# Linear attention and a SwiGLU block in fp32: k^T v of the next block in two visits per up phase

## The chip, the cores and the metric

The kernel runs on one core of one Trainium2 chip. The metric is device time in microseconds, median of three runs: 1023.67 (1023.01 to 1025.28). The trace shown below comes from an execution with a span of 1021.4 us. All data are fp32.

## What is computed

The reference, cut to what matters: a linear attention without softmax and with an RMS norm per head, then a gated feed-forward block on the result, read as 4608 tokens of width 512.

```python
# q, k, v: (8, 8, 576, 64);  g_norm: (64,);  w_gate, w_val: (512, 1536);  w_out: (1536, 512)
kv  = np.einsum('bhsd,bhse->bhde', k, v)
o   = np.einsum('bhsd,bhde->bhse', q, kv)
x   = o / np.sqrt(np.mean(o * o, axis=-1, keepdims=True) + 1e-6) * g_norm
x   = x.transpose(0, 2, 1, 3).reshape(4608, 512)
g   = x @ w_gate
out = (g / (1 + np.exp(-g)) * (x @ w_val)) @ w_out
```

## The kernel before

The 4608 tokens are cut into nine blocks of 512. A sequence has 576 tokens, so a block of tokens lies across two sequences, and blocks of k^T v (one for each of the eight sequences) are numbered as the blocks are. Each block n goes through an up phase (x times w_gate and w_val, then silu and the product h) and a down phase (h times w_out). The attention of block n+1 is worked into the phases of block n: k^T v in the up phase (`kv`, L305 to L323), q times k^T v, norm and the turning of x in the down phase (`steps`, L502).

The products of the feed-forward block are not the plain ones. From block 1 on, each is split into 2 x 2 pieces and done with seven products in place of eight (Winograd's form), with sums of operands and results on VectorE, GpSimd and ScalarE. `CHAIN` (L533) lists the seven; products 1, 6, 7 and 4 share a PSUM tile b, 5 and 3 a tile c, and 2 has a tile a. Block 0 has the plain products (`plain_up`, L1023). Block 1 has one level in the up phase (class `Up`, L587, products at L565). From block 2 on (`DEEP`, L540) the up phase has two levels (class `Inner`, L660, products at L728): 12 units, each of an outer product or two, whose weight leaves are read from DRAM into tiles t of a pool of nine (`Stream`, L787, loads at L809). In block 1 VectorE also makes these leaves (`leaf_steps`, L829) and SyncE stores them (L837). The down phase has one level in all blocks (class `Down`, L855, at L565), with products in the order 1, 6, 5, 7, 2, 4, 3 or 1, 5, 6, 7, 2, 4, 3 (L999).

k^T v of one block: eight heads in four pairs, nine slices of 64 rows each, products of 64 x 64 (L316). `kv(0)` is pairs 0 and 1, `kv(1)` is pairs 2 and 3; each has 9 x 2 x 2 = 36 products. Both write two PSUM tiles m, and after `kv(1)` ScalarE copies them out (L323). k and v come through tiles ld (a pool of four, which q uses too): the loads for `kv(1)` (`load_kv(1)`, L266) are in the source behind `kv(0)`.

In the up phase of block n (L968) a loop runs over the units, and after a third and two thirds of them calls `fill[4]` and `fill[8]`, which are `third` (L1109) and `two_thirds` (L1113). This is the order of the source. The order in the queue of each engine is decided when the program is built: a scheduler takes the instructions that its own estimate holds ready, so a group of products need not stay together or stand where the source has it. `tc.issue_after(ins)` binds what is traced inside it to be queued behind `ins` on `ins`'s own engine; it adds no wait on a semaphore.

In the program of before the products at L316 stand on TensorE as follows; "down" is the down phase of block n-1, between its products 2 and 4, "third" and "two thirds" are the places of the source. The 72 products for block 1 stand together ahead of the down phase of block 0 and are outside this table and outside the change.

| up phase n (k^T v of block n+1) | visits, in products |
|---|---|
| 1 | 17 down, 19 third, 36 two thirds |
| 2 | 17 down, 19 third, 29 in the unit before two thirds, 7 two thirds |
| 3, 4, 5 | 17 down, 19 third, 36 two thirds |
| 6 | 17 down, 8 and 11 in the first unit, 36 two thirds |

Phases 7 and 8 have none, since there are eight sequences.

Of the kernel before, what the change touches and what calls it, by code (L numbers as in the profile page):

```python
# [18 lines left out]
def kernel(  # L19
# [41 lines left out]
    nc = tc.nc  # L61

    B, H, S, D = q.shape
# [55 lines left out]
    class Words:  # L119
# [12 lines left out]
        def __init__(self, src, shape):  # L132
            self.raw = ld_pool.tile([P, LD], U32, name="ld")[:, 0 : 2 * BLK]
            dst = self.raw.rearrange("p (a b) -> p a b", a=shape[0])
            self.sent = nc.sync.dma_start(out=dst, in_=src)
            self.shape = shape
            self.begun = False
# [55 lines left out]
    class Att:  # L193
# [111 lines left out]
        def kv(self, g):  # L305


            if self.n == B:
                return
            if g == 0:  # L310
                self.kv_ps = [m_psum.tile([P, 2, D], F32, name="m") for _ in range(2)]
            for c in range(KT):
                for r in range(2):
                    k, v = self.k[2 * g + r], self.v[2 * g + r]
                    for u in range(2):
                        nc.tensor.matmul(  # L316
                            self.kv_ps[r][u * D : (u + 1) * D, g, :], lhsT=k[:, u, c, :], rhs=v[:, u, c, :],
                            start=(c == 0), stop=(c == KT - 1),
                        )
            if g == 1:  # L320
                dst = kvs[self.n % 3].rearrange("p (g r) d -> p r g d", r=2)
                for r in range(2):
                    nc.scalar.copy(out=dst[:, r], in_=self.kv_ps[r])  # L323
# [220 lines left out]
    class Quad:  # L544
# [11 lines left out]
        def multiply(self, p):  # L556
            name, first = CHAIN[p]
            if first:
                tiles = [PSUMS[name].tile([P, 2, HB], F32, name=name) for _ in range(1 + (name in self.apart))]
                self.ps[name], self.apart[name] = tiles[0], tiles[-1]  # L560
            banks = self.ps[name], self.apart[name]
            for e, i in self.order(p):
                lhsT, rhs = self.operands(p, e, i)

                nc.tensor.matmul(  # L565
                    banks[e][:, e], lhsT=lhsT, rhs=rhs, start=first and i == 0 and (e == 0 or banks[0] is not banks[1]),
                    stop=i == self.steps - 1, skip_group_check=True,
                )
            getattr(self, f"after{p}", lambda: None)()
# [90 lines left out]
    class Inner:  # L660
# [58 lines left out]
        def multiply(self, p):  # L719
            if p == 1:  # L720
                self.begin()
            name, first = CHAIN[p]
            if first:
                self.ps[name] = PSUMS[name].tile([P, 2, 2, P], F32, name=name)
            ps = self.ps[name][:, 0 : len(self.outers)]
            for i, o in enumerate(self.outers):
                for f in range(2):
                    nc.tensor.matmul(  # L728
                        ps[:, i, f], lhsT=self.weight(o, p, f), rhs=self.operand(o, p),
                        start=first and (i, f) == (0, 0), stop=True, skip_group_check=True,  # L730
                    )
            if p in self.ADDED:
                e, q = self.ADDED[p]
                dst = self.dst[:, :, :, e, q]
                add(nc.vector, dst, ps, dst)
            else:
                e, q = self.MADE[p]
                dst = self.dst[:, :, :, e, q]
                if self.onto:
                    add(nc.vector, dst, ps, self.onto(e, q))  # L740
                else:
                    nc.scalar.copy(out=dst, in_=ps)  # L742
            if p in (2, 7, 3, 4):
                getattr(self, f"made{self.g}", lambda *_: None)(p, e, q)
            stream.pump()
# [196 lines left out]
    class Ffn:  # L942
        def __init__(self, n, att):
            self.n, self.att = n, att
            self.h = h_pool.tile([P, NF, BLK], F32, name="h")
            self.ps, self.leaf_room, self.ended, self.owed = {}, None, None, None

            self.making, self.later, self.latest = [], [], []

        def store(self, o, t, columns=slice(None)):  # L950
            rows = out[BLK * self.n : BLK * (self.n + 1), columns].rearrange("(t p) d -> p t d", t=T)
            nc.sync.dma_start(out=rows[:, t : t + o.shape[1], :], in_=o)
# [15 lines left out]
        def up(self, fill):  # L968

            self.s1 = s_pool.tile([P, NP, HB], F32, name="s1")  # L970
            units = []
            for d in range(NP // 2):
                if self.n < DEEP:
                    units += [Up(self, 2 * d), Up(self, 2 * d + 1)]
                else:
                    shared = {}
                    units += [Inner(self, d, g, shared) for g in range(4)]
            units[0].prepare()
            last = None
            for i, this in enumerate(units):  # L980
                if i + 1 < len(units):
                    units[i + 1].prepare()
                for unit, p in this.sequence(last):
                    if unit:
                        unit.multiply(p)
                        self.make(4)
                last = this
                fill.get(12 * (i + 1) // len(units), lambda: None)()
            self.down_ = Down(self)
            self.down_.turn_t(5)  # L990
            for unit, p in last.sequence(None):
                if unit is None:
                    last.multiply(p)
# [86 lines left out]
    for n in range(NB):  # L1080
        ffn = Ffn(n, blocks[n])
        nxt = blocks[n + 1] if n + 1 < NB else None
# [23 lines left out]
                nxt.kv(g)  # L1106
        else:

            def third():  # L1109
                nxt.kv(0)  # L1110
                nxt.load_kv(1)

            def two_thirds():  # L1113
                nxt.kv(1)
                if nxt.n == 2:
                    for i in range(2):
                        nxt.load_q(i)

            fill = {4: third, 8: two_thirds} if nxt else {}
            if n == DEEP:  # L1120
                for a, at in enumerate((1, 2, 3, 5)):
# [50 lines left out]
```

## Time and profile before

| what | value |
|---|---|
| time, median of 3 | 1023.67 us |
| span of the traced execution | 1021.4 us |
| TensorE busy | 1006.0 us, 98% |
| VectorE busy | 701.1 us, 69% |
| GpSimd, ScalarE busy | 369.0 and 227.9 us |
| records of L316 on TensorE | 1008, two for each product, 217 to 268 ns each, up to four at once |
| granted TensorE clock | 1.000 |
| HBM traffic | 138.02 MB read, 22.41 MB written, 157 GB/s over the span |

The duration of a record of TensorE is that of one product from its issue to its end, and products overlap in the pipeline. What a group costs is therefore read from starts: the time from the start of one group to the start of the next. In the timeline, instructions of one line and form are merged, with the count behind; a group's printed duration runs to the end of its last product and overlaps the next group. Idle time is printed in brackets with what ended it, and only where the records leave a gap. The busy share of TensorE is an upper bound for its work for the same reason: records of a product that waits inside the array count as busy.

### The profile page before, as it was taken

The numbers are of one execution on the slowest core, as the hardware profiler recorded it, in microseconds if no ns is written. First come the engines' busy times: TensorE is split into PE (matmuls) and PEld (weight loads), VectorE is DVE, ScalarE is ACT, GpSimd is POOL, SyncE is SP. The second block draws the span as 40 slices with busy tenths as digits, with TensorE's granted clock in tenths as the row PEclk, the third lists the DMA queues.
The fourth block names the chain that finished last, engine by engine and source line by source line (L and its number), as shares of the span: only waits on it lengthen the run. The fifth ranks groups of instructions, "written<-read, shape, count | busy, mean of one in ns | idle before, by whom it ended". The sixth has DMA issues, their size and how long they took to land.

```text
span 1021.4 us, 21409 instructions
## 1 busy us (share of the span) xinstructions
PE 1006.0 (98%) x8522; PEld 897.1 (88%) x8522; DVE 701.1 (69%) x1169; ACT 227.9 (22%) x353; POOL 369.0 (36%) x280
## 2 busy tenths in 40 slices
PE   6999999999999999999999999999999999999998
PEld 4544688888999989998999899988998999989997
DVE  2999688998665946685558566665669466946661
ACT  2765112121211221121121211111121211221110
POOL 0000263534055503561246315630555045513670
PEclk9999999999999999999999999999999999999999
DMA  8689643767888377845686568636772766066601
GB/s 237 203 255 271 124 77 108 187 165 156 250 210 255 60 176 203 252 92 129 209 238 144 96 195 247 177 60 201 231 199 46 177 195 190 22 167 201 191 27 42
DMA packets 273845, 170.26 MB, mean 167 GB/s; under 512 B 150609, under 2 KB 241873, under 8 KB 273745
## 3 DMA queue, kind: packets, MB, share of 16 engines
q1 hardware_dynamic: 238800, 164.42, 59.3%
q10 hardware_dynamic: 34880, 4.46, 2.7%
q8 instruction: 68, 1.11, 0.4%
q14 instruction: 33, 0.26, 0.1%
q0 software_dynamic: 64, 0.00, 0.0%
HBM read 138.02 MB, written 22.41 MB: 157 GB/s over the span
## 4 chain that ended last, share of the span: by engine, by line
PE 90%; DVE 6%; DMA 2%; issue 1%; ACT 1%; SPq 0%; DVEq 0%; ACTq 0%
PE b L728 26%; PE b L565 19%; PE c L728 13%; PE c L565 10%; PE a L728 6%; PE a L565 5%; PE b L1032 4%; PE c L1032 4%; PE m L316 2%; PE m L361 1%; DVE r L112 1%; DVE xi L112 1%; DVE r L111 1%; DMA h<-in_v_dram 1%; DVE t L112 1%
## 5 line engine op out<-in xcount | busy, mean ns | idle before, releaser
L111 POOL TENSOR_TENSOR r<-r 128x256 f32<-128x256 f32 (+1 forms) x105 | 110.8, 1061 | 300.9 <-DVE r L111 272.2
L111 DVE TENSOR_TENSOR r<-b,r 128x512 f32<-128x512 f32 (+1 forms) x273 | 161.9, 606 | 65.5 <-PE b L728 60.1
L112 POOL TENSOR_TENSOR t<-wo 128x512 f32<-128x512 f32 x81 | 114.5, 1438 | 212.4 <-DVE wo L111 102.9
L111 DVE TENSOR_TENSOR r<-c,r 128x512 f32<-128x512 f32 (+1 forms) x179 | 108.5, 617 | 89.0 <-PE c L728 54.8
L728 PE MATMUL b<-x,t 128*128 128x128 f32 x1092 | 151.3, 276 | 0.0
L111 DVE TENSOR_TENSOR r<-a,r 128x512 f32<-128x512 f32 (+1 forms) x99 | 62.5, 631 | 113.4 <-PE a L565 70.7
L728 PEld LDWEIGHTS b<-x,t 128*128 128x128 f32 x1092 | 136.5, 192 | 0.8
L728 PE MATMUL c<-xi,t 128*128 128x128 f32 x840 | 112.4, 276 | 0.4 <-DVE xi L111 0.4
L113 POOL TENSOR_TENSOR h<-r 128x1024 f32<-128x1024 f32 (+1 forms) x40 | 82.3, 2072 | 76.9 <-DVE r L111 73.9
L728 PEld LDWEIGHTS c<-xi,t 128*128 128x128 f32 x840 | 102.9, 192 | 0.5 <-DVE xi L111 0.5
L565 PE MATMUL b<-wo,h 128*128 128x256 f32 x432 | 100.1, 383 | 0.1
L565 PE MATMUL b<-t,h 128*128 128x256 f32 x432 | 96.9, 381 | 0.0
L565 PEld LDWEIGHTS b<-t,h 128*128 128x128 f32 x432 | 81.6, 190 | 11.3 <-issue 0.2
L565 PEld LDWEIGHTS b<-wo,h 128*128 128x128 f32 x432 | 79.9, 190 | 13.1 <-DVE h L113 2.5
L742 ACT COPY r<-b 128x512 f32<-128x512 f32 x63 | 36.9, 585 | 211.6 <-PE b L728 211.6
L728 PE MATMUL b<-xi,t 128*128 128x128 f32 x588 | 79.8, 276 | 0.0
L728 PEld LDWEIGHTS b<-xi,t 128*128 128x128 f32 x588 | 72.4, 192 | 0.0
L728 PE MATMUL b<-x,wg 128*128 128x128 f32 x336 | 52.7, 279 | 0.2 <-DVE x L112 0.2
L728 PE MATMUL b<-x,wv 128*128 128x128 f32 x336 | 51.4, 276 | 0.0
L565 PE MATMUL a<-wo,h 128*128 128x256 f32 x216 | 48.3, 379 | 0.0
L565 PE MATMUL c<-t,s 128*128 128x256 f32 x216 | 48.1, 380 | 0.0
L565 PE MATMUL c<-wo,h 128*128 128x256 f32 x216 | 48.1, 379 | 0.0
(133 smaller groups left out, 1565.7 us busy)
## 6 DMA issues: line engine op xcount, KB each, us to landing
t<-w SPq DMA_DIRECT2D x336, 256.0 KB, 3.6
out_dram<-r SPq DMA_DIRECT2D x17, 512.0 KB, 3.1
ld<-in_k_dram SPq DMA_DIRECT2D x26, 288.0 KB, 5.2
ld<-in_v_dram SPq DMA_DIRECT2D x26, 288.0 KB, 5.9
ld<-in_moe_w_gate_dram SPq DMA_DIRECT2D x12, 512.0 KB, 4.8
ld<-in_moe_w_val_dram SPq DMA_DIRECT2D x12, 512.0 KB, 4.7
ld<-in_moe_w_out_dram SPq DMA_DIRECT2D x12, 512.0 KB, 4.9
w<-t SPq DMA_DIRECT2D x18, 256.0 KB, 3.0
```

The source lines that it names most:

```text
L111: add = lambda e, o, a, b: e.tensor_tensor(out=o, in0=a, in1=b, op=OP.add)
L112: sub = lambda e, o, a, b: e.tensor_tensor(out=o, in0=a, in1=b, op=OP.subtract)
L113: mul = lambda e, o, a, b: e.tensor_tensor(out=o, in0=a, in1=b, op=OP.mult)
L316: nc.tensor.matmul(self.kv_ps[r][u * D : (u + 1) * D, g, :], lhsT=k[:, u, c, :], rhs=v[:, u, c, :], start=(c == 0), stop=(c == KT - 1),)
L361: self.multiplied = nc.tensor.matmul(self.ps[i][u][p : p + D, t, j, :], lhsT=self.qt[rows, 2 * i + t, j, p : p + D], rhs=kvs[b % 3][rows, ...
L565: nc.tensor.matmul(banks[e][:, e], lhsT=lhsT, rhs=rhs, start=first and i == 0 and (e == 0 or banks[0] is not banks[1]), stop=i == self.ste ...
L728: nc.tensor.matmul(ps[:, i, f], lhsT=self.weight(o, p, f), rhs=self.operand(o, p), start=first and (i, f) == (0, 0), stop=True, skip_group ...
L742: nc.scalar.copy(out=dst, in_=ps)
L1032: nc.tensor.matmul(t, lhsT=w[f // 2][:, i, P * (f % 2) : P * (f % 2 + 1)], rhs=x[:, i, of], start=(i == 0), stop=(i == NS - 1),)
```

## The change

k^T v of the next block is to be kept in two visits per up phase. Two bounds are put on the queue of TensorE. `visit(g)` traces `kv(g)` inside an `issue_after` on the last product that was traced before it (`ffn.multiplied`, set at L565 and L728), so its products can't be queued ahead of that one. And where the visited block is one with k^T v (`nxt.n < B`), the last product of `kv(g)` (`positions`) is kept in `ffn.visited`, and the next unit's product in `up` is traced inside an `issue_after` on it, so it can't be queued ahead of the end of the visit. Nothing is computed differently.

```diff
@@ kv
-                        nc.tensor.matmul(
+                        self.positions = nc.tensor.matmul(
@@ Quad.multiply
-                nc.tensor.matmul(
+                self.ffn.multiplied = nc.tensor.matmul(
@@ Inner.multiply
-                    nc.tensor.matmul(
+                    self.ffn.multiplied = nc.tensor.matmul(
@@ Ffn.__init__
+            self.visited = None
@@ Ffn.up
                     if unit:
-                        unit.multiply(p)
+                        visited, self.visited = self.visited, None
+                        with tc.issue_after(visited.ins) if visited else ExitStack():
+                            unit.multiply(p)
                         self.make(4)
@@ the loop over blocks
+            def visit(g):
+                with tc.issue_after(ffn.multiplied.ins):
+                    nxt.kv(g)
+                if nxt.n < B:
+                    ffn.visited = nxt.positions
+
             def third():
-                nxt.kv(0)
+                visit(0)
                 nxt.load_kv(1)
 
             def two_thirds():
-                nxt.kv(1)
+                visit(1)
```

In the built program the visits are then 36 at the third and 36 at two thirds in each of the phases 1 to 6: 12 in place of 20. The order on VectorE and ScalarE stays as it was. On GpSimd two neighbours change places in phase 1 (an h and a t of the last unit). On SyncE, in phase 1 two loads of q move behind two stores of leaves each; in phase 2 one load of q moves ahead of the loads of k and v, and the later loads of k move ahead of two loads of t; in phase 6 the four loads of k and v for `kv(1)`, which lay spread between loads of t from the start of the phase, stand together behind the first visit, as they do in phases 2 to 5.

## The prediction

> **What bounds the kernel now.** I read the page first: busy time of the engines, then the chain that ended last.
>
> ```profile
> PE 1006.0 (98%) x8522; PEld 897.1 (88%) x8522; DVE 701.1 (69%) x1169; ACT 227.9 (22%) x353; POOL 369.0 (36%) x280
> PE 90%; DVE 6%; DMA 2%; issue 1%; ACT 1%; SPq 0%; DVEq 0%; ACTq 0%
> ```
>
> TensorE works 98% of the span at full granted clock, and 90% of the last chain is its own. So the time is the length of TensorE's queue, plus the few places where it waits. k^T v is 2% of the chain (PE m L316), but what counts is what a visit to it costs the products around it. I therefore read TensorE's timeline around every visit. Columns: start, duration, instruction, count; the trace has two records for each product of the source, so a visit "x34" is 17 products. Phase 3 (the products of block 3, with k^T v of block 4 between them) has the three sizes that matter: 17 in the down phase before it, 19 and 36 in its up phase.
>
> ```profile
> 362.93 5.34 PE L565 MATMUL a<-wo,h 128*128 128x256 f32 x24
> 368.21 0.79 PE L316 MATMUL m<-ld 64*64 64x64 f32 x34
> 368.93 5.45 PE L565 MATMUL b<-t,h 128*128 128x256 f32 x24
> 374.21 5.34 PE L565 MATMUL c<-wo,h 128*128 128x256 f32 x24
> ...
> 398.69 1.06 PE L728 MATMUL b<-xi,t 128*128 128x128 f32 x8
> 399.68 0.81 PE L316 MATMUL m<-ld 64*64 64x64 f32 x38
> 400.41 0.71 PE L728 MATMUL b<-x,wg 128*128 128x128 f32 x4
> 400.96 0.61 PE L728 MATMUL b<-x,t 128*128 128x128 f32 x4
> ...
> 421.51 1.06 PE L728 MATMUL b<-xi,t 128*128 128x128 f32 x8
> 422.49 1.28 PE L316 MATMUL m<-ld 64*64 64x64 f32 x72
> 423.70 0.71 PE L728 MATMUL b<-x,wg 128*128 128x128 f32 x4
> 424.25 0.61 PE L728 MATMUL b<-x,t 128*128 128x128 f32 x4
> ```
>
> Starts give the price. Undisturbed, the 24 records of a down product take 5.18 us from start to start (352.57, 357.75, 362.93) and four L728 records 0.447. From 362.93 to 374.21 are 11.28 us, 0.92 more than two down products: the 17 cost 0.92. From 398.69 to 400.96 are 2.27, against 3 x 0.447 = 1.34: the 19 cost 0.93. From 421.51 to 424.25 are 2.74: the 36 cost 1.40. So 17 more products in one visit cost 0.47, or 0.028 each, and 0.93 - 19 x 0.028 = 0.40 us is a price per visit, whatever its size. It shows on both sides: 0.1 us before, 0.1 us in the first product after (0.71 instead of 0.61), 0.2 us inside.
>
> **What the skill says.** The Trainium skill, "TensorEngine Tiling", Key Properties: "Changing tiling mode (not just tile) drains the TensorE". A visit changes from 128 x 128 to 64 x 64 tiles and back. The page gives no price; the trace agrees with the sentence, and the 0.40 us is its price here. The skill, "GPSIMD Engine Reference", Specifications, says that GpSimd shares its SBUF interfaces with VectorE when a VectorE instruction has two SBUF inputs. The trace agrees: in phase 1, 128x256 subtractions of VectorE that alone take 0.42 us take up to 1.4 beside a GpSimd instruction. That matters for phase 1 only, where VectorE never rests.
>
> **The change, part by part.** By the order of the built programs, the before has 20 visits in six phases: 17, 19, 36 in phases 1, 3, 4, 5; 17, 19, 29, 7 in phase 2; 17, 8, 11, 36 in phase 6. After has 12, each of 36, at the places where the 19 and the last piece stand in the other phases. The same 432 products run; eight changes of mode go, 8 x 0.40 = 3.2 us if TensorE bounds everywhere. I go through the phases, since a visit can stand where TensorE would wait.
>
> *Phases 3, 4, 5:* no wait of TensorE in the trace near any visit. 0.92 + 0.93 - 1.40 = 0.45 saved in each, 1.35 together.
>
> *Phase 2:* the visit of 29 stands between products at 308.61 and 310.77: 2.16 less 2 x 0.447 is 1.27. The 7 cost 1.93 - 1.34 = 0.59. Sum 0.92 + 0.93 + 1.27 + 0.59 - 2 x 1.40 = 0.91 saved, if the weight tiles are there. I matched each weight load's landing to the first product that reads the tile: the closest around this place land 2.37 (t read at 310.22), 2.44 and 2.9 us ahead. TensorE comes 0.45 earlier up to here (0.92 less 0.47) and 1.7 after the 29 are gone. Even if no transfer moves, 2.37 covers it. So 0.91.
>
> *Phase 1:* VectorE makes the leaves of the weights, and from 168.3 to 223 its instructions follow one another with hardly a pause; TensorE meets it:
>
> ```profile
> 191.87 1.89 PE L565 MATMUL b<-x,t 128*128 128x256 f32 x8
> 193.96 2.00 PE L565 MATMUL c<-x,wv 128*128 128x256 f32 x8 [0.20 <-DVE r L111]
> ```
>
> Eight records take 1.727, so TensorE stood 0.36 here; at 208.00 it stood 0.44 and at 230.31 again. VectorE's run begins behind products of TensorE (it waits 1.65, 2.17, 0.40, 0.38 us for them from 157.97 to 168.26), and the 17 at 143.5 lie ahead of those. So their 0.92 moves the whole run forward. The 0.47 that the 19 grow by at 175.5 falls into TensorE's 0.36 and 0.44 of waiting: nothing. Two GpSimd instructions (a t of unit 5 and an h) change places there, and two q loads go behind w stores: the same work on both, no sum. 0.92 saved; bounds 0 (the run held by something else) and 0.92.
>
> *Phase 6:* the 8 and the 11 stand where the sums of x are late.
>
> ```profile
> 704.56 0.46 PE L316 MATMUL m<-ld 64*64 64x64 f32 x16
> 704.95 0.71 PE L728 MATMUL b<-x,wv 128*128 128x128 f32 x4
> ...
> 706.15 0.69 DVE L111 TENSOR_TENSOR r<-b,r 128x512 f32<-128x512 f32 x1
> 706.76 1.08 DVE L111 TENSOR_TENSOR xi<-x 128x896 f32<-128x896 f32 x1
> 706.93 0.57 PE L316 MATMUL m<-ld 64*64 64x64 f32 x22
> 707.89 2.05 PE L728 MATMUL c<-xi,t 128*128 128x128 f32 x16 [0.39 <-DVE xi L111]
> ```
>
> Without the 8, the product that r<-b at 706.15 waits for ends 0.59 earlier, but VectorE is busy up to 705.95 (x at 705.35 plus 0.60): 0.20 gained. Without the 11 TensorE only waits longer for xi. The 17 of the down phase are a true gain, since the activation x<-x follows the copy of product 4 at 697.70, behind TensorE. The 36 that replace them stand later, in full work. 0.92 + 0.20 - 1.40 = -0.28: this phase loses 0.28. Bounds: -0.48 (no 0.20) and +0.5.
>
> *The loads:* k and v of pairs 2 and 3 are issued when the first visit ends, as in phase 5 before; in phase 6 they were spread and now come together ahead of weight loads. In phase 5 tiles behind such a group land 1.72 us or more ahead of use. Weight loads that queue behind the k loads on SyncE wait for the visit's end; TensorE, on which they wait, is as late as they are. Nothing.
>
> *The two queue edges* (issue_after) bind instructions of TensorE to one another only; no wait on another engine comes in. What stands behind a visit is the next up product, and it was there before.
>
> Sum: 0.92 + 0.91 + 1.35 - 0.28 = 2.90 saved. 1023.67 - 2.90 = 1020.8.
>
> **Rivals.**
> *The visits of phases 1 and 2 stood in waits* (VectorE's run is held by its stores, not by TensorE; tiles of phase 2 come late). For it: the chain of phase 1 goes through stores ("DMA w<-r", 3.2 us at 220.9), and a DMA share of 0.9 to 1.0 in phase 2. Against it: 2.37 us of margin, and the stores follow VectorE. Only phases 3 to 6 count: -1.35 + 0.28 = -1.07, 1022.6, no change that can be measured.
> *More than that:* phase 6 hides its 36 as the others hide theirs, and 3.2 are saved, with 0.47 hidden in phase 1 on top: 3.67, 1020.0. Against it: the 0.39 wait above.
> *Slower: the bigger visits hold the loads.* A first visit of 36 lets k and v loads go later, weight tiles behind them come late. If in each of phases 2 to 6 TensorE waits 1 us, 5 - 2.9 = 2.1 are lost: 1025.8. For it: in phases 2 and 5 margins are only 1.9 and 1.7 us; in phase 3 the four k and v loads land 1.1 to 1.4 us apart. Against it: loads and TensorE shift together.
>
> **How the numbers follow.** Chances: forecast 0.60, no change 0.22, more 0.12, slower 0.06. The time is the forecast's. Low end 1019.5: the "more" case less the 0.6 by which runs of before lie under their median. High end 1023.4: the "no change" case plus 0.8 of the same scatter. 0.2% is 2.05 us, that is 1021.6; the forecast lies 0.85 beyond it, so I give a small part of it (0.04) to no change: faster 0.68, same 0.26, slower 0.06.
>
> **What would show it.** Right: each visit is x72 with about 1.4 us around it; TensorE's busy instructions unchanged in number; the first product of each phase earlier by 0.92 (phase 2: 1.8 with phase 1's), phases 3 to 5 shorter by 0.45, phase 6 with a wait of about 1.4 us for xi. Wrong: a wait for a t tile after a visit (slower), the wait at 193.96 grown to 1 us (phase 1 held by VectorE), or a visit of 36 that costs more than 1.4.

## The result, and the profile after

The changed kernel takes 1021.02 us in the median of five runs (1020.91 to 1021.33), the kernel before 1023.82 beside it (1023.01 to 1025.28, five runs). The ratio is 0.997, with an interval of 0.9958 to 0.9982: faster by 2.8 us. Predicted were 2.90 less and 1020.8.

From the page of the changed kernel, the busy times (the shares of the chain are those of the kernel before):

```profile
PE 1003.5 (98%) x8522; PEld 895.9 (88%) x8522; DVE 700.9 (69%) x1169; ACT 228.1 (22%) x353; POOL 368.9 (36%) x280
```

As many instructions as before on every engine, and 2.5 us less on TensorE. The same place as before, phase 3, in TensorE's timeline (start, duration, instruction, count; the trace has two records for each product):

```profile
396.38 1.06 PE L728 MATMUL b<-xi,t 128*128 128x128 f32 x8
397.37 1.28 PE L316 MATMUL m<-ld 64*64 64x64 f32 x72
398.58 0.71 PE L728 MATMUL b<-x,wg 128*128 128x128 f32 x4
399.12 0.61 PE L728 MATMUL b<-x,t 128*128 128x128 f32 x4
...
419.67 1.06 PE L728 MATMUL b<-xi,t 128*128 128x128 f32 x8
420.66 1.28 PE L316 MATMUL m<-ld 64*64 64x64 f32 x72
421.87 0.71 PE L728 MATMUL b<-x,wg 128*128 128x128 f32 x4
422.41 0.61 PE L728 MATMUL b<-x,t 128*128 128x128 f32 x4
```

Two visits of 36 products, the same from start to start: 396.38 to 399.12 are 2.74 us, less 3 x 0.447 is 1.40. The visit of 17 in the down phase is gone.

To see where the time went, cut the trace at one instruction that every block has: the first record of product 2 of the down phase (a<-wo,h). Stretch n runs from that of the down phase of block n-1 to that of block n, so it holds all visits of phase n. Microseconds between these starts in the two traces:

| | up to the first | stretch 1 | 2 | 3 | 4 | 5 | 6 | 7 | 8 |
|---|---|---|---|---|---|---|---|---|---|
| before | 138.22 | 116.22 | 108.49 | 107.78 | 107.78 | 107.73 | 109.36 | 104.53 | 96.99 |
| after | 138.17 | 115.78 | 107.60 | 107.33 | 107.33 | 107.28 | 109.74 | 104.52 | 96.99 |
| measured change | -0.05 | -0.44 | -0.89 | -0.45 | -0.45 | -0.45 | +0.38 | -0.01 | 0 |
| predicted | 0 | -0.92 | -0.91 | -0.45 | -0.45 | -0.45 | +0.28 | 0 | 0 |

The traces differ by 2.4 us, the medians by 2.8; the changed kernel timed again (e11 below) lies 2.5 under the kernel before it was timed beside. Stretches 2 to 5 are as forecast to 0.02 us. Phase 1 gave half of what was put down for it, and phase 6 lost 0.10 more. Why phase 1 fell short is the one question left by the result; the price of a visit and the loss of phase 6 were only read from one trace, so they are tested too.

In phase 1, the wait at 208.00 in the kernel before, and then the two waits of TensorE over 0.2 us that are left in the changed kernel:

```profile
208.00 1.99 PE L565 MATMUL c<-x,wv 128*128 128x256 f32 x8 [0.28 <-DVE r L111]
```
```profile
207.58 1.99 PE L565 MATMUL c<-x,wv 128*128 128x256 f32 x8 [0.72 <-DVE r L111]
229.82 1.99 PE L565 MATMUL c<-x,wv 128*128 128x256 f32 x8 [0.25 <-DVE r L111]
```

The product at 193.96 of before comes at 193.10, and its wait of 0.36 is gone under the growth of the visit, as forecast. But the one that came at 208.00 comes at 207.58: 0.42 earlier, not 0.86. Somewhere between the two VectorE lost 0.4 us. Here is its timeline there, with GpSimd's:

```profile
198.68 0.42 DVE L112 TENSOR_TENSOR wv<-wv 128x256 f32<-128x256 f32 x1
199.13 1.38 DVE L111 TENSOR_TENSOR wv<-wv 128x256 f32<-128x256 f32 x1
200.43 0.68 DVE L111 TENSOR_TENSOR r<-c,r 128x512 f32<-128x512 f32 x1
201.03 2.08 DVE L112 TENSOR_TENSOR xi<-wv 128x512 f32<-128x512 f32 x2
```
```profile
198.88 1.35 POOL L112 TENSOR_TENSOR t<-wg,wv 128x512 f32<-128x512 f32 x1 [1.25 <-DVE r L112]
201.19 1.64 POOL L113 TENSOR_TENSOR h<-r 128x512 f32<-128x512 f32 x1 [0.96 <-DVE r L111]
```

The addition wv<-wv at 199.13 takes 1.38 us beside GpSimd's t. The same instructions in the kernel before, VectorE's and then GpSimd's:

```profile
200.02 0.42 DVE L111 TENSOR_TENSOR wv<-wv 128x256 f32<-128x256 f32 x1
200.36 0.68 DVE L111 TENSOR_TENSOR r<-c,r 128x512 f32<-128x512 f32 x1
200.96 2.57 DVE L112 TENSOR_TENSOR xi<-wv 128x512 f32<-128x512 f32 x2
```
```profile
200.19 1.39 POOL L112 TENSOR_TENSOR t<-wg,wv 128x512 f32<-128x512 f32 x1 [1.67 <-DMA w<-t]
201.53 1.72 POOL L113 TENSOR_TENSOR h<-r 128x512 f32<-128x512 f32 x1
```

There t waited for a store to land and began 0.17 us after the addition had; now it begins as soon as VectorE's r is there, 0.25 ahead of the addition. VectorE comes to the addition 0.89 us earlier than before, to r<-c 0.07 later, and leaves xi<-wv 0.42 earlier, since that one is shorter by 0.49. This is 12 us behind the pair on GpSimd that the change exchanges (186.65 and 188.31 in the changed kernel), which costs a little too: VectorE's xi<-wv beside it takes 1.29 us at 185.94, 1.16 in the kernel before.

In phase 6 the wait for xi was 0.39 and is 1.04:

```profile
702.38 0.61 PE L728 MATMUL a<-x,wg 128*128 128x128 f32 x4
704.03 2.05 PE L728 MATMUL c<-xi,t 128*128 128x128 f32 x16 [1.04 <-DVE xi L111]
```

### The profile page after: what moved, and what is told of

The parts are those of the page before. It is cut to its first block, busy times and chain, and to the rows that moved or that the text cites. A ratio compares the mean times of both kernels' runs of the same rounds, so it can differ in the third digit from the quotient of the medians.

```text
span 1019.1 us, 21397 instructions
## 1 busy us (share of the span) xinstructions
PE 1003.5 (98%) x8522; PEld 895.9 (88%) x8522; DVE 700.9 (69%) x1169; ACT 228.1 (22%) x353; POOL 368.9 (36%) x280
## 4 chain that ended last, share of the span: by engine, by line
PE 90%; DVE 6%; DMA 2%; issue 1%; ACT 1%; SPq 0%; DVEq 0%; ACTq 0%
PE b L728 26%; PE b L565 19%; PE c L728 13%; PE c L565 10%; PE a L728 6%; PE a L565 5%; PE b L1035 4%; PE c L1035 4%; PE m L361 1%; PE m L316 1%; DVE r L112 1%; DVE r L111 1%; DVE xi L112 1%; DMA h<-in_v_dram 1%; DVE t L112 1%
## 5 line engine op out<-in xcount | busy, mean ns | idle before, releaser
L728 PE MATMUL b<-x,t 128*128 128x128 f32 x1092 | 151.2, 275 | 0.0
L728 PEld LDWEIGHTS b<-x,t 128*128 128x128 f32 x1092 | 136.5, 192 | 0.8 <-DVE r L111 0.2
L728 PE MATMUL c<-xi,t 128*128 128x128 f32 x840 | 112.4, 275 | 1.0 <-DVE xi L111 1.0
L728 PEld LDWEIGHTS c<-xi,t 128*128 128x128 f32 x840 | 102.9, 192 | 1.2 <-DVE xi L111 1.2
L565 PE MATMUL b<-wo,h 128*128 128x256 f32 x432 | 100.1, 383 | 0.1
L565 PE MATMUL b<-t,h 128*128 128x256 f32 x432 | 96.2, 379 | 0.0
L565 PEld LDWEIGHTS b<-t,h 128*128 128x128 f32 x432 | 82.0, 190 | 11.3 <-issue 0.2
L565 PEld LDWEIGHTS b<-wo,h 128*128 128x128 f32 x432 | 79.8, 190 | 13.2 <-DVE h L113 2.5
L728 PE MATMUL b<-xi,t 128*128 128x128 f32 x588 | 79.7, 276 | 0.0
L728 PEld LDWEIGHTS b<-xi,t 128*128 128x128 f32 x588 | 72.4, 192 | 0.0
L728 PE MATMUL b<-x,wg 128*128 128x128 f32 x336 | 52.8, 279 | 0.2 <-DVE x L112 0.2
L728 PE MATMUL b<-x,wv 128*128 128x128 f32 x336 | 51.2, 275 | 0.0
L565 PE MATMUL a<-wo,h 128*128 128x256 f32 x216 | 48.3, 379 | 0.0
L565 PE MATMUL c<-t,s 128*128 128x256 f32 x216 | 48.1, 379 | 0.0
L565 PE MATMUL c<-wo,h 128*128 128x256 f32 x216 | 48.1, 379 | 0.0
```

Source lines behind the costliest of these rows:

```text
L565: self.ffn.multiplied = nc.tensor.matmul(banks[e][:, e], lhsT=lhsT, rhs=rhs, start=first and i == 0 and (e == 0 or banks[0] is not banks[1 ...
L728: self.ffn.multiplied = nc.tensor.matmul(ps[:, i, f], lhsT=self.weight(o, p, f), rhs=self.operand(o, p), start=first and (i, f) == (0, 0), ...
```

## The experiments

Stretches of all of them, from their traces, beside the changed kernel:

| | up to the first | 1 | 2 | 3 | 4 | 5 | 6 |
|---|---|---|---|---|---|---|---|
| changed kernel | 138.17 | 115.78 | 107.60 | 107.33 | 107.33 | 107.28 | 109.74 |
| the same again (e11) | 139.57 | 115.90 | 107.60 | 107.33 | 107.33 | 107.29 | 109.75 |
| GpSimd's t bound behind the addition (e1) | 138.50 | 115.01 | 107.60 | 107.33 | 107.33 | 107.29 | 109.75 |
| phase 6 unbound (e2) | 138.07 | 115.41 | 107.60 | 107.33 | 107.33 | 107.29 | 109.47 |
| the same again (e10) | 140.17 | 115.95 | 107.60 | 107.33 | 107.33 | 107.28 | 109.47 |
| visit of phase 6 early (e3) | 139.56 | 115.82 | 107.60 | 107.33 | 107.33 | 107.28 | 108.89 |
| e1 and e3 together (e4) | 138.74 | 114.98 | 108.39 | 107.33 | 107.33 | 107.29 | 109.91 |
| four visits (e5) | 139.25 | 115.88 | 108.31 | 108.04 | 108.04 | 107.99 | 110.33 |
| whole-array products (e6) | 138.22 | 115.37 | 108.81 | 108.55 | 108.55 | 108.50 | 110.96 |
| one visit (e7) | 139.91 | 118.61 | 107.03 | 106.98 | 108.81 | 107.02 | 109.27 |
| phase 1 unbound (e8) | 141.32 | 115.54 | 107.60 | 107.33 | 107.33 | 107.28 | 109.63 |
| one visit from phase 2 on (e9) | 138.69 | 115.80 | 107.84 | 106.98 | 107.83 | 106.93 | 109.27 |

The time up to the first cut varies by 3 us between executions although nothing in it differs: at its start TensorE waits for v to land (the longest such wait is 3.0 us in the changed kernel, 3.8 in the kernel before, 5.1 in e10), and in e1, e8 and e11 it also stands there for 1.2 to 1.6 us with no cause named. These waits do not account for all of the 3 us. So the stretches say more than the total does.

**e5 and e6: what is a visit's price?** e5 cuts each visit in two, of 20 and 16 products, with one up product between them; nothing is left out.

```diff
-            def visit(g):
+            def visit(g, slices):
                 with tc.issue_after(ffn.multiplied.ins):
-                    nxt.kv(g)
+                    nxt.kv(g, slices)
             def third():
-                visit(0)
+                visit(0, range(5))
+                ffn.rest = rest_0       # visit(0, range(5, KT)), called behind the next up product
```

> The changed kernel with each visit of 36 cut into 20 and 16, one product of the up phase between them: 24 visits in place of 12, the same 432 products. Theory (a visit has a price of 0.40 us whatever its size): stretches 3, 4, 5 grow from 107.33 by 2 x 0.40 to 108.1, stretch 2 from 107.60 to 108.4, stretch 6 from 109.74 to 110.5; the whole is up to 4.8 us longer than the changed kernel, 1025.4, ratio to before 1.002. Rival (the odd cuts at 17, 19, 29 and 7, which part a pair of products, were what cost; even cuts cost nothing): all stretches as in the changed kernel, 1021.

Measured: 1025.31 us (median of 20; before 1023.98 beside it), ratio 1.0014 (1.0007 to 1.002). From 398.27 to 403.15 in phase 3 are 4.88 us:

```profile
398.27 1.06 PE L729 MATMUL b<-xi,t 128*128 128x128 f32 x8
399.26 0.81 PE L317 MATMUL m<-ld 64*64 64x64 f32 x40
400.00 0.71 PE L729 MATMUL b<-x,wg 128*128 128x128 f32 x4
400.55 0.61 PE L729 MATMUL b<-x,t 128*128 128x128 f32 x4
401.09 0.69 PE L317 MATMUL m<-ld 64*64 64x64 f32 x32
401.71 1.60 PE L729 MATMUL c<-xi,t 128*128 128x128 f32 x12
403.15 0.61 PE L729 MATMUL c<-xi,wv 128*128 128x128 f32 x4
```

The 28 records of up products take 28 x 0.1117 = 3.13 (0.447 / 4 = 0.1117), so 36 k^T v products in two visits cost 1.75, against 1.40 in one. Stretches 3 to 5 are longer by 0.71 for two visits more: 0.35 each. The time per visit is there, a little smaller than the 0.40 of the prediction. The rival, that only the odd cuts of the kernel before cost, is out: these cuts are even and part no pair.

e6 asks whether it is the change of the tile or only that another group comes between. Each visit makes nine products of 128 x 128 instead of 36 of 64 x 64. The part left out is k^T v itself: what is computed in its place is of no use.

```diff
-            for c in range(KT):
+            if self.n > 1:
+                k, v = self.whole_kv[g, 0], self.whole_kv[g, 1]
+                for c in range(KT):
+                    self.positions = nc.tensor.matmul(
+                        self.kv_ps[g].rearrange("p g d -> p (g d)"), lhsT=k[:, P * c : P * (c + 1)],
+                        rhs=v[:, P * c : P * (c + 1)], start=(c == 0), stop=(c == KT - 1),
+                    )
+            for c in range(KT) if self.n == 1 else ():
```

> The changed kernel with other products in the visits of phases 1 to 6: nine of 128 x 128 in the full array, from the same k and v tiles, in place of 36 of 64 x 64. It leaves k^T v of these blocks out (the products mix heads), so that a visit needs no change of the array's tiling. A product of 128 x 128 takes 2 x 0.1117 in the up phase, nine take 2.01. Theory (the 0.40 is the change of tiling and back): a visit costs 2.01 and no more, stretches 3, 4, 5 are 107.33 + 2 x (2.01 - 1.40) = 108.55. Rival (the 0.40 belongs to any interruption of the up products, another PSUM tile or other operands): a visit costs 2.41, stretches 3, 4, 5 are 109.35.

Measured: 1026.56 us in one run, stretches 3 to 5 of 108.5 to 108.55.

```profile
397.24 1.06 PE L736 MATMUL b<-xi,t 128*128 128x128 f32 x8
398.13 2.17 PE L316 MATMUL m<-ld 128*128 128x128 f32 x18
400.14 0.61 PE L736 MATMUL b<-x,wg 128*128 128x128 f32 x4
400.59 0.61 PE L736 MATMUL b<-x,t 128*128 128x128 f32 x4
```

398.13 to 400.14 are 2.01 us, which is 18 x 0.1117. There is nothing over: no 0.1 us ahead of the group, and the first product after it is at 0.61, not 0.71. So it is the change between 128 x 128 and 64 x 64 that costs, as the Trainium skill has it ("TensorEngine Tiling (Array Packing)", Key Properties: a change of the tiling mode drains TensorE), and a group of 128 x 128 in the same place costs nothing over its own products. That the cost is a drain is the skill's word; the traces show where it lies and how large it is. (e6 is slower than the changed kernel because nine whole-array products take 2.01 us where 36 small ones take 1.40 with their price.)

**e7 and e9: one visit instead of two.** If the price is per visit, joining the last two saves it once more. e7 makes both halves at the third. The second half reads k and v of the first half, since those of pairs 2 and 3 are not yet loaded; that part of the computation is left out, the loads and the number of products stay.

```diff
-                    k, v = self.k[2 * g + r], self.v[2 * g + r]
+                    j = r if self.n > 1 else 2 * g + r
+                    k, v = self.k[j], self.v[j]
             def visit(g):
-                    nxt.kv(g)
+                    nxt.kv(0)
+                    nxt.kv(1)
             def two_thirds():
-                visit(1)
```

> The changed kernel with one visit of 72 at the third in place of two of 36; the second half reads the tiles of pairs 0 and 1 again, so pairs 2 and 3 are left out of k^T v (their loads are kept). Theory (0.40 a visit, 0.028 a product): a visit of 72 costs 0.40 + 72 x 0.028 = 2.40 in place of 2 x 1.40, stretches 3, 4, 5 fall from 107.33 to 106.9, the whole by 6 x 0.40 = 2.4 us to 1018.6, ratio 0.9948. Rival (large visits cost more, since what stands behind them waits longer): stretches 3 to 5 at 107.3 or more.

Measured: 1024.03 us (median of 12), ratio 0.9999 (0.9991 to 1.0008). The forecast of the time missed by 5.4 us. The price is as said:

```profile
400.40 1.06 PE L729 MATMUL b<-xi,t 128*128 128x128 f32 x8
401.38 2.33 PE L317 MATMUL m<-ld 64*64 64x64 f32 x144
403.64 0.71 PE L729 MATMUL b<-x,wg 128*128 128x128 f32 x4
404.19 0.61 PE L729 MATMUL b<-x,t 128*128 128x128 f32 x4
...
512.68 0.49 PE L729 MATMUL b<-x,wg 128*128 128x128 f32 x3 [1.68 <-issue]
```

400.40 to 404.19 less 3 x 0.447 are 2.45 us for 72 products, 0.35 less than two visits of 1.40; stretches 3 and 5 are shorter by 0.35 and 0.26. The loss is elsewhere. In phase 4, behind the first record after the visit, TensorE stands for 1.68 us until 512.68, and the profile's lines name nothing that it waited for. And in phase 1 the scheduler, with the visits placed otherwise, has put loads of q ahead of stores of leaves on SyncE, and a store that VectorE needs lands late; that the loads are the reason is likely, but no run moved them alone. VectorE's timeline:

```profile
194.10 1.27 DVE L112 TENSOR_TENSOR xi<-wg 128x512 f32<-128x512 f32 x1 [3.37 <-DMA w<-xi]
```

TensorE's at the next place, and a window behind it (columns: window, length, busy of PE, PEld, DVE, ACT, POOL, then the granted TensorE clock, DMA share, GB/s):

```profile
211.25 3.63 PE L566 MATMUL c<-x,wv 128*128 128x256 f32 x8 [2.14 <-DVE r L111]
```
```profile
212.00:214.00 2.00, 2.00 (x7) 1.55 (x6) 1.93 (x6) 0.00 (x0) 0.91 (x1) 0.50 0.57 159
```

VectorE is late with r, TensorE waits 2.14 us for it, and then runs at a granted clock of 0.50 (1.00 in the window 208 to 210): its eight records take 3.47 us from start to start (211.25 to 214.72) instead of 1.73. A wait of 2.1 us has cost nearly 4. Not every execution has this: of the twelve runs six have a mean granted clock of 0.998, as the traced one has, and take 1024.9 us on average; the other six have 0.999 or 1.000 and take 1023.5. So the clock is a small part of the 5.4 us.

e9 takes phase 1 out of the question: it joins the visits from phase 2 on only, and has the order of the changed kernel on every engine up to phase 2.

```diff
-                    k, v = self.k[2 * g + r], self.v[2 * g + r]
+                    j = r if self.n > 2 else 2 * g + r
+                    k, v = self.k[j], self.v[j]
             def visit(g):
-                    nxt.kv(g)
+                    if nxt.n == 2 or g == 0:
+                        nxt.kv(g)
+                    if nxt.n > 2 and g == 0:
+                        nxt.kv(1)
             def two_thirds():
-                visit(1)
+                if nxt.n == 2:
+                    visit(1)
```

> Phases 2 to 6 make both halves of k^T v in one visit of 72 products at the third; phase 1 keeps its two visits of 36, and with them the order of the changed kernel on every engine. As in the kernel with one visit in all phases, the second half reads k and v of the first (pairs 0 and 1 in place of 2 and 3), so that part of the computation is left out; all loads are made. Theory (price of a visit 0.35 to 0.40 us, and the loss of the kernel with one visit in every phase came from its phase 1, where q loads went ahead of the stores of leaves, and from pauses that are not the visits'): stretch 1 of 115.0 to 115.8, stretch 2 107.0, 3 to 5 107.0 each, 6 109.3; 5 x 0.35 = 1.75 less than the changed kernel, about 1019.3 us, ratio to the kernel before 0.9955. Rival (a visit of 72 itself makes TensorE stop, as once at 512.68 for 1.68 us): stretches 2 to 6 of 108 to 109, and 1021 us or more.

Measured: 1021.02 us (median of five), ratio 0.9967 (0.9954 to 0.9979); the changed kernel on the same chip 1021.43 (e11). Stretch 1 is that of the changed kernel again (115.80), so the loss of e7 there came with the order of its phase 1. Stretches 3, 5 and 6 are shorter by 0.35, 0.35 and 0.47. But stretches 2 and 4 are longer by 0.24 and 0.50:

```profile
306.42 0.68 PE L729 MATMUL c<-xi,t 128*128 128x128 f32 x4 [0.24 <-DMA t<-w]
```
```profile
508.46 0.49 PE L729 MATMUL b<-x,wg 128*128 128x128 f32 x3 [0.69 <-issue]
```

In phase 2 two weight tiles come late, at 305.46 and 306.42; from start to start they cost 0.22 and 0.41 us. In phase 4 TensorE stands at the same instruction as in e7, one record behind the visit. Neither the theory (1.75 less) nor the rival (a stop behind every visit of 72) holds: the price is saved in three phases, and of the two in which it is not, one waits for tiles and the other stops for a cause that the profile's lines do not name.

The traces hold more about it, in their records of DMA packets: 68 transfers of 16 KB on queue 8 in every trace but that of e6 (63), of a kind called instruction. The 32nd of them lands at 511.26 in e7 and at 507.02 in e9, and TensorE goes on 1.42 and 1.44 us later, both times with its record 4124. In the ten other traces with all products of k^T v of 64 x 64 the 32nd lands 6.2 to 10.1 us ahead of the start of that record, and none of them stops there. The three stops at the start (e1, e8, e11) end 1.43 to 1.56 us behind the first such transfer, all at record 221. So these stops of TensorE go with late transfers of its own instructions. No run moved such a transfer, so that it is the cause is argued, and why it came late in phase 4 of e7 and e9 stays open.

**e1 and e8: what held phase 1?** Theory: GpSimd's t, which now lies beside an addition of VectorE. e1 makes that t wait for the addition.

```diff
-                sub(nc.gpsimd, t[-1], b, t2)
+                turned = sub(nc.gpsimd, t[-1], b, t2)
+            if j == NP - 1:
+                tc.add_manual_dep(
+                    turned.ins, leaf_sums[2, 6].ins.name,
+                    mybir.DependencyInfo(mybir.DependencyClass.Sync, mybir.DependencyReason.DATA), reason="order",
+                )
```

> The changed kernel with one wait more: GpSimd's last t of unit 5 in phase 1 waits for VectorE's addition on wv that precedes r<-c (the one that took 1.38 us at 199.13 in the changed kernel, 0.42 before). The order on every engine is that of the changed kernel. Stretches are counted from product 2 of one down phase to product 2 of the next; stretch 1 was 116.22 us before and 115.78 with the change. Theory (GpSimd's subtraction came 0.45 us too early against VectorE's run and met that addition): the addition takes 0.42 again, VectorE's r<-c keeps its lead of 0.9, and stretch 1 is 115.3. Rival (the run loses the half microsecond anyway, at another instruction, or is held by its stores): stretch 1 stays at 115.7 to 115.8. The other stretches stay at 107.60, 107.33, 107.33, 107.28, 109.74, 104.52.

Measured: 1020.49 us in one run, stretch 1 of 115.01. VectorE's timeline of e1:

```profile
199.52 0.43 DVE L111 TENSOR_TENSOR wv<-wv 128x256 f32<-128x256 f32 x1
199.87 0.68 DVE L111 TENSOR_TENSOR r<-c,r 128x512 f32<-128x512 f32 x1
200.47 2.94 DVE L112 TENSOR_TENSOR xi<-wv 128x512 f32<-128x512 f32 x2
```

The addition takes 0.43 again, but xi<-wv behind it takes 2.94 instead of 2.08: of the 0.95 regained, 0.86 is lost there, and TensorE still stands 0.63 for r ahead of 207.87. So t beside the addition is not the cause in the sense of the theory: GpSimd and VectorE share time here either way, and the loss goes to the instruction that meets GpSimd's. In all three traces xi<-wv ends 0.28 us behind GpSimd's h: at 203.53 and 203.25 in the kernel before, 203.11 and 202.83 in the changed one, 203.41 and 203.13 in e1. So when VectorE leaves this place goes with when GpSimd does, and h (which follows t, and waits for r<-c in the changed kernel) ends only 0.42 earlier in the changed kernel. The loss is not one execution's: behind this place, counted from the first cut, VectorE is 0.32 to 0.38 us ahead of the kernel before in the changed kernel, e2, e3, e9, e10 and e11, and 0.40 to 0.44 in e1 and e4, which have the edit; ahead of the pair on GpSimd it was 0.91 to 0.93 in all eight. That GpSimd contends with instructions of VectorE that have two SBUF inputs is in the Trainium skill ("GPSIMD Engine Reference", Specifications), and the trace agrees: 0.42 us alone, 1.38 beside t. Stretch 1 did become shorter, but later, and mostly for another reason. The kernel before and the changed one have a line on VectorE that e1 has without its wait. First of the kernel before, then of the changed one:

```profile
220.91 1.03 DVE L112 TENSOR_TENSOR xi<-wv 128x512 f32<-128x512 f32 x2 [0.69 <-DMA w<-xi]
```
```profile
220.41 1.03 DVE L112 TENSOR_TENSOR xi<-wv 128x512 f32<-128x512 f32 x2 [0.63 <-DMA w<-xi]
```

VectorE waits there for a store of leaves to land before it may write the tile again. The store stands on SyncE behind 16 loads of q. Where these took 7.9 us to issue (e1, e4, e6, e8) there is no such wait; where they took 9.0 to 9.5 (the kernel before, the changed one, e2, e3, e9, e10, e11) VectorE waits 0.44 to 0.74. Why the issue takes longer in some executions is open.

e8 undoes the change in phase 1 alone: its order there is that of the kernel before, on every engine.

```diff
             def visit(g):
+                if nxt.n == 2:
+                    nxt.kv(g)
+                    return
                 with tc.issue_after(ffn.multiplied.ins):
```

> The changed kernel with phase 1 left without the two bounds, so that its visits are 17, 19 and 36 as before; VectorE, GpSimd and SyncE have the order of before in phase 1. Stretch 1 was 116.22 in the one trace of before and 115.78, 115.41 and 115.82 in three traces of the changed program. Theory (the change is worth 0.4 to 0.8 in stretch 1): 116.2. Rival (stretch 1 varies from run to run by as much, since VectorE waits there for a store): under 115.9. Stretches 2 to 6 as in the changed kernel in both cases.

Measured: 1023.63 us in one run, whose start alone was 3.2 us later than the changed kernel's; stretch 1 of 115.54. Taken as it is, that is less than the changed kernel's 115.78, as the rival has it. But e8 had no wait for the store. Stretch 1 less that wait:

| | stretch 1 | wait for w<-xi | the rest |
|---|---|---|---|
| order of before: before | 116.22 | 0.69 | 115.53 |
| order of before: e8 | 115.54 | none | 115.54 |
| order of after: after | 115.78 | 0.63 | 115.15 |
| order of after: e11 | 115.90 | 0.67 | 115.23 |
| order of after: e10 | 115.95 | 0.74 | 115.21 |
| order of after: e3 | 115.82 | 0.61 | 115.21 |
| order of after: e9 | 115.80 | 0.59 | 115.21 |
| order of after: e2 | 115.41 | 0.44 | 114.97 |

The two executions with the old order agree to 0.01 us once the wait is taken off, the six with the new one lie from 114.97 to 115.23; e1, which has the new order and its edit, has no wait and 115.01. So the change is worth 0.3 to 0.6 us in phase 1, and the store's landing moves the stretch by up to 0.7 beside it. This assumes that a wait lengthens the stretch by its own length, which fits these eight but was not tested by itself.

**e2, e10 and e3: phase 6.** Theory: phase 6 loses because 8 and 11 products stood where TensorE waits for xi. e2 leaves the bounds out in phase 6 alone (`if nxt.n == 7: nxt.kv(g); return` at the head of `visit`), e10 is the same kernel timed.

> The changed kernel with phase 6 left without the two bounds, so that its k^T v stands as before: 17 in the down phase, 8 and 11 in the first unit, 36. Theory (in phase 6 the 8 and the 11 stood in TensorE's wait for xi, so keeping them together costs 0.38 there): stretch 6 is 109.36 as before, in place of 109.74, and stretches 1 to 5 stay at 115.78, 107.60, 107.33, 107.33, 107.28. Rival (the phase became longer through the loads of k and v that moved behind the first visit): the order of the loads goes back too, so this run alone does not part them, but a wait for a t tile would have to be seen in the changed kernel; the next run parts them.

Measured in e2: stretch 6 of 109.47, and the wait for xi is again 0.39:

```profile
703.74 0.57 PE L316 MATMUL m<-ld 64*64 64x64 f32 x22
704.70 2.05 PE L728 MATMUL c<-xi,t 128*128 128x128 f32 x16 [0.39 <-DVE xi L111]
```

The loads of k and v go back to their old places too, but phase 6 of the changed kernel has no wait for a weight tile, so it is not they that cost.

> The changed kernel with the queue bounds left out in phase 6 alone, timed beside the others. Theory (phase 6 loses by the bounds, since 8 and 11 products stood in TensorE's waits there): 0.27 us below the changed kernel, 1020.7 us, stretch 6 of 109.4 to 109.5, the rest as in the changed kernel; too little to tell the two by runs. Rival (the gain in the first trace of this kernel was chance): stretch 6 of 109.7.

Measured in e10: 109.47 again, but 1022.21 us in the median of 21 runs (1020.1 to 1023.86), ratio 0.9981 (0.9974 to 0.9988). The stretch is as the theory has it in both executions, the time is not: it lies 0.8 above that of the changed kernel beside it, and the intervals of the two ratios overlap. The total varies by more than a quarter of a microsecond (the start alone is 138.07 in e2 and 140.17 in e10), so it cannot show the gain.

e3 goes further and puts the whole visit of 36 into that wait, by making products 1 and 2 of the first two units ahead of it:

```diff
+            if self.early and i < 2:
+                a, b = units[0:2]
+                return [
+                    [(a, 1), (a, 2), (b, 1), (b, 2), ("visit", self.early), (a, 5), (a, 6), (a, 7)],
+                    [(b, 5), (a, 3), (b, 6), (a, 4), (b, 7)],
+                ][i]
```

> The changed kernel, but in phase 6 the first visit of 36 is put whole into the wait for xi: units 1 and 2 do products 1 and 2 first, then the visit, then the rest. Theory (TensorE waits there 1.04 us and more, a visit costs 1.40, and nearly all of it is hidden): the wait of 1.04 for xi is gone or under 0.1, and stretch 6 falls from 109.74 to 108.3 to 108.6, below the 109.36 of before. Rival (the wait only moves behind the visit, since VectorE's sums come later too, or the loads of k and v set the phase): stretch 6 stays at 109.3 or more.

Measured: 1021.5 us in one run; stretch 6 of 108.89, 0.85 less than the changed kernel.

```profile
704.36 1.28 PE L316 MATMUL m<-ld 64*64 64x64 f32 x72
705.57 1.60 PE L728 MATMUL c<-xi,t 128*128 128x128 f32 x12
708.16 0.68 PE L728 MATMUL b<-x,wg 128*128 128x128 f32 x4 [0.99 <-DVE x L112]
```

The wait for xi is gone, as the theory has it, but 0.99 us of it has come back one instruction further, as a wait for x, of which 0.20 was there before. So less was gained than expected.

**e4: the two together**, e1's and e3's edits in one kernel.

> The edits of the first and third run of this group together. Theory: 0.45 from stretch 1 and 1.2 from stretch 6 off the 1021.0 of the changed kernel, 1019.4 us, ratio to before 0.9957. Rival (neither holds): 1021.0, ratio 0.9973.

Measured: 1021.15 us (median of nine, 1019.1 to 1022.89), ratio 0.9964 (0.9951 to 0.9977), not to be told from the changed kernel. Its trace has two waits that neither part had alone:

```profile
309.70 1.13 PE L733 MATMUL c<-xi,t 128*128 128x128 f32 x8 [0.57 <-DMA t<-w]
```
```profile
723.77 0.71 PE L733 MATMUL b<-x,t 128*128 128x128 f32 x4 [0.41 <-DMA t<-w]
```

k and v and the weight tiles behind them landed later: in phase 2 the first k load was issued at 291.15 and landed at 298.5 (after: 291.38 and 296.25), and tiles that had landed by 303.1 landed by 305.7. Stretch 2 lost 0.79, though phase 2 has the order of the changed kernel, and phase 6 lost the gain of e3. So no kernel here beats the changed one by what can be measured.

**e11: the changed kernel once more**, on the chip of e9 and e10.

> The changed kernel itself once more, on the chip of the other two. Theory (stretch 1 differs between executions by the landing of stores; the other stretches don't): stretch 1 anywhere from 115.0 to 115.8, stretch 2 107.6, 3 to 5 107.3, 6 109.7, the time 1020.9 to 1021.3 in the median. Rival (stretch 1 is fixed by the program): 115.8 again within 0.1.

Measured: 1021.43 us (median of nine, 1020.8 to 1023.11), ratio 0.9978 (0.9968 to 0.9987). Stretches 2 to 6 are the same to 0.01; stretch 1 is 115.90 against 115.78, so the rival's 0.1 is just missed, and the theory's spread is seen only with e2 (115.41).

**Which bound does it?** In the built programs, a kernel with the lower bound alone (the visit queued behind the last up product) has the order of the changed kernel on every engine, and one with the upper bound alone (`ffn.visited`) has that of the kernel before. So the first `issue_after` does all of this, and the second does nothing here. Neither of the two was run.

## Why the prediction was right, point by point

**The price of a visit** (0.028 us for a product and 0.40 for a visit): shown, with a corrected size. Three ways to visit at the same place of phase 3, 36 in one, 36 in two, and 72 in one, cost 1.40, 1.75 and 2.45: 0.029 for a product and 0.35 for a visit. With products of the whole array instead of 64 x 64 tiles the price is nil (e6). For the sums it made no difference, since the costs of 0.92, 0.93 and 1.40 were read off whole.

**Phases 3, 4, 5** (0.45 each): 0.45 each. **Phase 2** (0.91, if the tiles are there): 0.89, with no wait for a tile. The margin of 2.37 us on which this stood did hold, but is not as safe as the prediction took it: in e4 and e9 TensorE stood 0.57 and 0.24 us for tiles of phase 2, in e4 with phase 2 as in the changed kernel.

**Phase 1** (0.92, bounds 0 and 0.92): mis-sized. 0.44 in the traces, 0.3 to 0.6 with the store's landing taken off. The step "their 0.92 moves the whole run forward" failed: VectorE's run isn't rigid. It was earlier by 0.97 us up to 186, by 0.86 to 0.89 from 188 to 199, and by 0.42 from 203 on. The prediction took the GpSimd side as "the same work on both, no sum", and looked only at the pair that changes places; but that exchange cost 0.1, and a GpSimd instruction further on started at another moment, and VectorE shares time with it. e1 shows that moving that one instruction doesn't bring the time back: the next one takes it. That VectorE's end there follows the end of GpSimd's h is seen in three traces; no run moved h alone, so it isn't more than that. The run of instructions that follow one another "with hardly a pause" also has a pause that the prediction passed over: 0.69 us for a store at 220.91, 0.63 in the changed kernel. VectorE leaves it 0.50 earlier and TensorE goes on at 229.82 in place of 230.31, 0.49 earlier; less the 0.05 of the start that is the 0.44 of the stretch. So the size of the gain also rests on when that store lands.

**Phase 6** (-0.28): the terms were right. The product that waits for xi starts 20.54 us behind the cut in the changed kernel (704.03 - 683.49) and 21.67 in the kernel before (707.89 - 686.22): 1.13 gained, where the sum had 0.92 + 0.20. The visit took 1.40 of it back, which leaves a loss of 0.27. The other 0.1 is lost at one up product at 741.70 that no step named (0.54 us to the next instead of 0.447). e2 has it too, so the visits of phase 6 don't make it; e8 has phase 6 as in the changed kernel without it, and its stretch is 109.63. The wait for xi was forecast as about 1.4 us and is 1.04. e2 undoes the bounds in this phase and gets 0.27 back, which is the -0.28.

**The loads** (nothing): right for the changed kernel, which has no wait over 0.2 us for a tile in phases 2 to 6. **The queue edges** (no wait on another engine): right, and one of the two is idle.

**The rivals.** "Phases 1 and 2 stood in waits" (1022.6) was half right for phase 1, and its reason, that VectorE's run is held by its stores, is seen at 220.9; it was wrong for phase 2. The sign named for it, a wait at 193.96 of 1 us, did not come there but at the next such product: 0.72 at 207.58, where it was 0.28. "More" (1020.0) fell with phases 1 and 6. "Slower, loads late" did not come in this kernel; e4 and e9 show that it was not far.

The sum of the traces is 2.36 less, not 2.90; the medians differ by 2.80, and by 2.53 with e11. The phases that were read off starts (2 to 5) came as forecast. That the total comes within 0.2 us of the measured one, with 0.48 missing in phase 1, is luck: the scatter from execution to execution made up for it.

## What to carry to other kernels

Read the price of an interruption from starts, with the group at two or three sizes between the same neighbours: the part that doesn't grow with the size is what joining groups saves. Then go through the places one by one, since a small group that stands in a wait is free, and joining it with one in full work costs. Where another engine runs without a pause, time given to its start need not arrive at its end; and before a gain of a few tenths of a microsecond is believed, cut the trace at an instruction that every version has, since the start of the kernel can vary by more.

## What was not expected of the hardware

- After a wait of 2.14 us TensorE ran at half the clock for eight records (0.43 us apart instead of 0.216; the clock record of e7 has 0.50 from 211.19 to 214.61). The Trainium skill ("TensorE: Matmul & The Clock Gate", Part 1) gives half the clock after at least one idle window of about 3.4 us; in this one trace a shorter wait was followed by it. Behind the waits of 0.72 and 1.04 us in the changed kernel, and behind the stop of 1.68 in e7, the clock stayed at 1.00.
- A 128 x 128 addition or subtraction of VectorE takes 0.28 us alone and 1.35 beside GpSimd (195.15 and 196.43 in the changed kernel), as long as a 128 x 256 one (0.42 and 1.38): the time beside GpSimd goes with GpSimd's instruction, of 1.31 to 1.35 us there, and hardly with the size of VectorE's.
- TensorE stopped for 1.68 and 0.69 us at the same instruction behind a visit of 72 (phase 4 of e7 and e9), for nothing that the profile's lines name. All five such stops over 0.35 us in the thirteen traces end 1.42 to 1.56 us after a 16 KB transfer of the kind instruction has landed.
